# Sharing TensorE clusters from an earlier group on, and placing stores and transposes later in one engine's order

## The chip, the cores and the metric

The kernel runs on one core of a Trainium2 chip. A core has five engines with an instruction stream each: TensorE (PE in the profile; PEld is its weight load), VectorE (DVE), ScalarE (ACT), GpSimd (POOL) and SyncE (SP), which in this kernel issues nearly all transfers. Each engine works through its stream in order. The metric is the time of one execution on the device in microseconds; lower is better. Seven runs of the kernel before have a median of 298.03 us and lie between 296.41 and 298.42.

## What is computed

The program is a retention layer followed by a two-layer network. Inputs q, k, v have 8 batches, 8 heads, 576 positions and a head size of 64; the weights are 512 x 2048 and 2048 x 512. All are float32.

```
scores = (q @ k^T) / sqrt(64)
ret    = (scores * Dmat) @ v          # Dmat[h, i, j] = gamma_h ** (i - j) for i >= j, else 0
x      = ret, heads side by side      # 4608 rows of 512
h      = x @ w_in                     # 4608 x 2048
g      = max(h, 0) ** 2
out    = g @ w_out                    # 4608 x 512
```

## The kernel before

**Units and groups.** The 4608 rows are 36 units of 128 rows: for each pair of batches eight "full" units (four of each batch) and a "tail" unit with the last 64 positions of both. Two units form a group, so there are 18 groups, numbered from 0. Each group goes through retention, then the first product with w_in, then relu and square, then the second product.

**Loads.** Units 0 to 7 (groups 0 to 3) are loaded in pairs and transposed on TensorE. From unit 8 on, `add_load` (line 273) issues k, q and v of each unit on SyncE, with a pool of five buffers of each; `add_unit` (line 347) casts k and q to half precision and multiplies v by decay factors on GpSimd (lines 353 and 365), and a DMA transpose on SyncE (`fx2`, line 376, issued at line 378) makes kqT, which holds k and q with the head size across partitions. Six such buffers exist.

**Retention.** It is done in chunks of 64 positions with a carried state, by small matmuls on 64 x 64 quarters of TensorE (`quad`, line 340). A unit has four parts: scores (k times q, line 561), sums (k times v for the state, line 571), output part 1 (state times q of the first kind, line 607), and output part 2 (masked scores times v and the rest of the state, line 612). VectorE masks the scores (`rT`, line 641), forms the states Rm, stmp and R (lines 660 to 670) and multiplies the output by decay factors into xT (line 702).

TensorE does these parts in clusters, each written as one task of the schedule, between 128-wide matmuls. Line 626 says which form a group has: `return JOIN <= g < last_g`, with `JOIN = 11` at line 228. A group that is not joined has a cluster with its own scores and sums (`fa`, line 727) and a later one with output part 1, a drain and output part 2 (`fb`, line 757). A joined group has a cluster with its output part 1 and the scores of the next group (`f1`, line 739), and one with the sums of the next group and its own output part 2 (`f2`, line 743); there is no drain in it, and the next group has no `fa` of its own. So before the change groups 4 to 10 are not joined, groups 11 to 16 are, and group 17, the last, has its output alone.

**The network.** `add_ff` (line 807) makes 64 matmuls with w_in for a group (line 825, tile ph), relu on ScalarE (line 833, rl), and squares on ScalarE or VectorE (lines 843 and 845, gT). From group 2 on the second product is one level of Strassen's scheme (`add_strassen`, line 878): VectorE forms four sums gS of gT blocks (line 891), TensorE makes seven products of eight matmuls each (line 914, tile po), and ScalarE and VectorE put the results together (lines 927, 937, 988). Each finished unit is stored by SyncE (`store`, line 790; lines 794 and 798), from four o tiles.

**The order.** Every piece of work is added to a `Schedule` (line 16) as a task with an engine, a key, an expected duration, the tasks that it depends on, buffers that it takes (`acq`), and an expected latency to other engines. `emit` (line 42) plays these durations through: an engine that is free takes, of the tasks whose data are expected to be there and whose buffers are free, the one with the lowest key. The order in which tasks are started there is the order in which each engine's instructions are written. On SyncE transposes have key -1, stores -0.5 and loads 0, so a transpose or store that is expected to be ready goes ahead of all loads. On the chip each engine keeps this order and waits for the data themselves.

Of the kernel before, what the change touches and what calls it, by code (L numbers as in the profile page):

```python
# [15 lines left out]
class Schedule:  # L16
# [4 lines left out]
        self.count = dict(count)  # L21
        self.tasks = []

    def add(self, eng, key, dur, fn, deps=(), acq=(), after=None):
        t = dict(eng=eng, key=key, dur=dur, fn=fn, acq=acq, n=len(self.tasks), users=[], free=[],
                 left=len(deps), ready=0.0, lat=self.LAT[eng] if after is None else after)
        for d in deps:
            d["users"].append(t)
        self.tasks.append(t)
        return t  # L30
# [11 lines left out]
    def emit(self):  # L42
        ready = {e: [] for e in self.LAT}
        busy = {e: False for e in self.LAT}
        events = []
        order = []
        seq = 0

        def push(at, what, t):
            nonlocal seq  # L50
            seq += 1
            heapq.heappush(events, (at, seq, what, t))
        for t in self.tasks:
            if t["left"] == 0:
                heapq.heappush(ready[t["eng"]], (t["key"], t["n"], t))
        now = 0.0
        while True:
            for e in ready:
                if busy[e]:
                    continue  # L60
                held = []
                while ready[e]:
                    item = heapq.heappop(ready[e])
                    t = item[2]
                    if all(self.count[r] >= t["acq"].count(r) for r in t["acq"]):
                        for r in t["acq"]:
                            self.count[r] -= 1
                        t["start"] = now
                        order.append(t)
                        busy[e] = True  # L70
                        push(now + t["dur"], "end", t)
                        break
                    held.append(item)
                for item in held:
                    heapq.heappush(ready[e], item)
            if not events:
                break
            now = events[0][0]
            while events and events[0][0] <= now + 1e-9:
                _, _, what, t = heapq.heappop(events)  # L80
                if what == "end":
                    busy[t["eng"]] = False
                    for w in t["users"]:

                        push(now + (0.0 if w["eng"] == t["eng"] else t["lat"]), "dep", w)
                    for g in t["free"]:
                        push(now + t["lat"], "free", g)
                elif what == "dep":
                    t["left"] -= 1
                    if t["left"] == 0:  # L90
                        heapq.heappush(ready[t["eng"]], (t["key"], t["n"], t))
                else:
                    t["left"] -= 1
                    if t["left"] == 0:
                        self.count[t["res"]] += 1
        assert len(order) == len(self.tasks)
        for t in order:
            t["fn"]()
# [3 lines left out]
def kernel(  # L102
# [122 lines left out]
    SQ_ACT = (0, 1, 2, 3, 4, 5, 6)  # L225
    SPREAD = 0.1
    SQ_LATE = (1, 4, 6)
    JOIN = 11
    LAG = {"v2": 1.2, "w1": 1.3, "k4": 0.7, "q4": 0.5}
    PAIRED = 8  # L230
    FIRST = ["k0", "q0", "v0", "k2", "q2", "w0", "v2", "w1", "w2", "w3", "w4", "w5", "w6", "w7", "k4", "q4", "v4", "k6", "q6", "v6"]
    sched = Schedule(dict(ff=4, prS=1, prO=1, g=3, ld=5, wst=4, kq=7, v16=7, rT=4, x=3, rl=3, o=4, p1=2, u2=2, u4=2,
                          R=6, Rm=6, kqT=6))
    add = sched.add
    tile_of = {}
# [99 lines left out]
    T = {}  # L335
# [11 lines left out]
    def add_unit(u, base):  # L347

        kind, b, c = units[u]
        tail = [tail_dec] if kind == "tail" else []  # L350

        def sorted_cast(op, out_, in_):
            op(out=out_.rearrange("p (n b a d) -> p n b a d", n=2, b=2, a=2),  # L353
               in_=in_.rearrange("p (n a b) d -> p n b a d", n=2, a=2))

        def fk():
            t = tile_of["kq", u] = cast.tile([P, 2, H * D], FP16, name="kq16", tag="kq16")
            sorted_cast(nc.gpsimd.tensor_copy, t[:, 0], tile_of["k32", u])

        def fq():  # L360
            sorted_cast(nc.gpsimd.tensor_copy, tile_of["kq", u][:, 1], tile_of["q32", u])

        def fv():
            t = tile_of["v16", u] = cast.tile([P, H, D], FP16, name="v16", tag="v16")
            nc.gpsimd.tensor_tensor(  # L365
                out=t, in0=tile_of["v32", u],
                in1=vdec[kind].rearrange("p (h o) -> p h o", o=1).to_broadcast([P, H, D]), op=ALU.mult)
        ck = add("POOL", base, 0.65, fk, deps=[loaded["k", u]], acq=("kq",))
        cq = add("POOL", base + 1, 0.62, fq, deps=[loaded["q", u], ck])
        cv = add("POOL", base + 2, 1.1, fv, deps=[loaded["v", u]] + tail, acq=("v16",))  # L370
        for what, t in (("k", ck), ("v", cv)):
            for w in gate.get((what, u), []):
                sched.need(w, t)
        T["casts", u] = [ck, cq, cv]
        sched.free("ld", [ck, cq, cv])
        def fx2():
            t = tile_of["kqT", u] = work.tile([P, 2 * NP, P], FP16, name="kqT", tag="kqT", bufs=6)
            nc.sync.dma_start_transpose(out=t, in_=tile_of["kq", u].rearrange("p x n -> p (x n)"))
        T["kqT", u] = [add("SP", -1, 2.7, fx2, deps=[ck, cq], acq=("kqT",), after=3.0)]

    def add_unit_pair(u, base):

# [239 lines left out]
    last_g = len(groups) - 1  # L622
# [167 lines left out]
    def store(u, o, lo=0, hi=DM, eng=nc.sync):  # L790
        kind, b, c = units[u]
        if kind == "full":
            r0 = b * S + c * P
            eng.dma_start(out=out[r0:r0 + P, lo:hi], in_=o[:, lo:hi])
        else:
            for i in range(2):
                r0 = (b + i) * S + 512
                eng.dma_start(out=out[r0:r0 + 64, lo:hi], in_=o[i * 64:(i + 1) * 64, lo:hi])
# [8 lines left out]
    def add_ff(g):  # L807
        us = groups[g]
        n = len(us)
# [8 lines left out]
        for fb in range(NF // nf):  # L818
            for j in range(nf):
                def f(fb=fb, j=j):  # L820
# [3 lines left out]
                    for m in range(NP):  # L824
# [3 lines left out]
                              deps=[T["x", u] for u in us] + wcast_of(nf * fb + j) + f1[-1:],  # L828
                              acq=("ff",) if j == 0 else ()))
# [26 lines left out]
        for s, u in enumerate(us):  # L856
            end = base2 + NF * (s + 1)
            f2 = T["ff2"][-1:] if s == 0 else f2[-1:]
            for fi in range(NF):
                def f(fi=fi, s=s, u=u):  # L860
                    if fi == 0:
                        tile_of["po", u] = ps_ff.tile([P, DM], FP32, name="po", tag="ff")
                    nc.tensor.matmul(tile_of["po", u], lhsT=tile_of["g", g][:, fi, s * P:(s + 1) * P],  # L863
                                     rhs=w_out16[:, fi, :], start=(fi == 0), stop=(fi == NF - 1))
                f2.append(add("PE", base2 + NF * s + fi, 0.216, f, deps=[sq[fi // nf]] + wcast[4 + fi // 4] + f2[-1:],
                              acq=("ff",) if fi == 0 else ()))

            def fo(u=u):
                tile_of["o", u] = o_pool.tile([P, DM], FP32, name="o", tag="o")
                nc.scalar.copy(out=tile_of["o", u], in_=tile_of["po", u])  # L870
            oc = add("ACT", end + 1, 0.59, fo, deps=[f2[-1]], acq=("o",))
            sched.free("ff", [oc])
            st = add("SP", -0.5, 0.7, lambda u=u: store(u, tile_of["o", u]), deps=[oc], after=2.5)
            sched.free("o", [st])
        sched.free("g", [f2[-1]])
        T["ff2"].append(f2[-1])
# [1 line left out]
    def add_strassen(g, us, base, sq):  # L878
# [51 lines left out]
        def o_tile(u):  # L930
            if ("o", u) not in tile_of:
                tile_of["o", u] = o_pool.tile([P, DM], FP32, name="o", tag="o")
            return tile_of["o", u]
# [63 lines left out]
        T["ff2"].append(p4)  # L997
        for u, ds in ((uA, [d11, c12]), (uB, [d22, d21])):
            if g < last_g:
                st = [add("SP", -0.5, 0.7, lambda u=u: store(u, o_tile(u)), deps=ds, after=2.5)]  # L1000
            else:
                st = []
                for d in ds:
                    lo = 0 if d in (d11, d21) else HM
                    eng = ("ACT", base + 25.1, 0.05) if d is d11 or d is d22 else ("SP", -0.5, 0.05)
                    st.append(add(*eng, lambda u=u, lo=lo, eng=eng: store(u, o_tile(u), lo, lo + HM,
                                                                          nc.scalar if eng[0] == "ACT" else nc.sync),
                                  deps=[d], after=2.5))
            sched.free("o", st)
# [44 lines left out]
```

## Time and profile before

| | value |
|---|---|
| median of seven runs | 298.03 us |
| profiled execution | 296.97 us |
| its span | 295.3 us |
| TensorE's granted clock | 0.998 |
| read from memory, written | 36.70 MB, 9.44 MB |
| share of the DMA engines, main queue | 83.1% |

The profile is one execution. The span runs from its first to its last instruction; 1.67 us of the execution lie around it. "Busy" is the time in which an engine has at least one instruction in work, as a share of the span. A row of who waited for whom has the total of the waits, how often, and the longest. In a row of instructions in order of time the first number is the start from the beginning of the span, the second the length of that run, and "x8" the number of instructions in it. The ends of matmuls are modelled, so the price of a group of matmuls is read from start to start.

### The profile page before, as it was taken

To read this page: it belongs to the slowest core of one execution; us is meant where nothing else is said; L and a number is where in the kernel's file an instruction comes from. 1 tells how busy PE (TensorE), PEld (TensorE's weight loads), DVE (VectorE), ACT (ScalarE), POOL (GpSimd) and SP (SyncE) were. 2 spreads that over 40 slices of the span, in tenths; PEclk is the share of its full clock that TensorE was granted. 3 is DMA by queue.
4 is the path that set the end of the run, shared out by engine and by line. 5 is a ranking of instruction groups with operands and counts; after the bars stand their busy time and mean duration, and the time that the engine had idled before them with its cause. 6 is when DMAs were issued, how large, how long until landed. Compare 5 with 4: busy or idle time off the path is not lost.

```text
span 295.3 us, 10076 instructions
## 1 busy us (share of the span) xinstructions
PE 284.3 (96%) x4328; PEld 234.6 (79%) x4328; DVE 200.6 (68%) x433; ACT 183.4 (62%) x347; POOL 95.5 (32%) x129
## 2 busy tenths in 40 slices
PE   7988999999989999999999999999999999999995
PEld 2557666687878888888888888788888888888884
DVE  4777489859494959493949587866668776464732
ACT  6256863485747675767576657657666677657830
POOL 4444374634243405162524232434141520000000
PEclk9999999999999999999999999999999999999999
DMA  7999999899998979899979799999899960201004
GB/s 205 327 372 386 362 259 235 191 224 164 219 172 204 184 161 189 207 195 205 191 174 165 173 173 211 206 169 213 126 230 179 204 163 2 74 2 71 2 0 144
DMA packets 139421, 54.14 MB, mean 183 GB/s; under 512 B 118128, under 2 KB 130928, under 8 KB 139376
## 3 DMA queue, kind: packets, MB, share of 16 engines
q1 hardware_dynamic: 139072, 53.23, 83.1%
q8 instruction: 34, 0.56, 0.9%
q10 hardware_dynamic: 304, 0.26, 0.3%
q14 instruction: 11, 0.09, 0.1%
HBM read 36.70 MB, written 9.44 MB: 156 GB/s over the span
## 4 chain that ended last, share of the span: by engine, by line
PE 79%; DVE 9%; DMA 5%; ACT 4%; issue 1%; POOL 1%; SPq 0%; DVEq 0%
PE ph L825 35%; PE po L914 30%; PE po L863 5%; PE psO L341 4%; DMA wo<-in_moe_w_out_dram 3%; DVE gS L891 3%; ACT gT L843 2%; PE psc L341 2%; DMA pair<-in_q_dram 2%; ACT rl L833 2%; PE psS L341 1%; PE warm L244 1%; PE psT L416 1%; DVE rT L641 1%; DVE R L670 1%
## 5 line engine op out<-in xcount | busy, mean ns | idle before, releaser
L825 PE MATMUL ph<-xT,w_in 128*128 128x256 f16 x1152 | 138.9, 273 | 1.2 <-POOL w_in L320 1.2
L825 PEld LDWEIGHTS <-w_in 128*128 128x128 f16 x1152 | 111.0, 98 | 16.8 <-POOL w_in L320 2.0
L833 ACT ACTIVATE rl<-ph 128x512 f16<-128x512 f32 x144 | 84.2, 588 | 48.3 <-PE ph L825 42.0
L843 ACT ACTIVATE gT<-rl 128x512 f16<-128x512 f16 x104 | 65.6, 631 | 3.1
L914 PEld LDWEIGHTS <-gS 128*128 128x128 f16 x512 | 49.4, 98 | 7.5 <-DVE gS L891 1.7
L914 PE MATMUL po<-wT,gS 128*128 128x256 f16 x384 | 52.1, 273 | 0.9 <-DVE gS L891 0.9
L891 DVE TENSOR_TENSOR gS<-gT 128x512 f16<-128x512 f16 x64 | 35.0, 547 | 20.7 <-ACT gT L843 20.6
L891 DVE TENSOR_TENSOR gS<-gT,gS 128x512 f16<-128x512 f16 x64 | 34.3, 537 | 21.8 <-ACT gT L843 21.1
L365 POOL TENSOR_TENSOR v<-v,vdec_full 128x512 f16<-128x512 f32 x24 | 26.7, 1113 | 62.8 <-DMA v<-in_v_dram 51.2
L914 PEld LDWEIGHTS <-gT 128*128 128x128 f16 x384 | 37.2, 98 | 4.9 <-issue 0.4
L914 PE MATMUL po<-w_out,gT 128*128 128x256 f16 x256 | 34.5, 273 | 0.0
L353 POOL CAST kq<-k 128x512 f16<-128x512 f32 x28 | 19.9, 710 | 28.4 <-DMA k<-in_k_dram 25.0
L845 DVE TENSOR_TENSOR gT<-rl 128x512 f16<-128x512 f16 x40 | 18.9, 475 | 14.8 <-ACT rl L833 14.1
L927 ACT COPY u<-po 128x256 f32<-128x256 f32 x32 | 11.8, 370 | 23.7 <-PE po L914 23.7
L353 POOL CAST kq<-q 128x512 f16<-128x512 f32 x28 | 18.7, 666 | 22.5 <-DMA q<-in_q_dram 22.0
L702 DVE TENSOR_TENSOR xT<-psO,gam_full 128x512 f16<-128x512 f32 x28 | 18.5, 683 | 3.7 <-PE psO L341 3.7
L641 DVE TENSOR_TENSOR rT<-psc,mask 128x512 f16<-128x512 f32 x28 | 18.6, 680 | 1.8 <-PE psc L341 1.8
L937 DVE TENSOR_TENSOR o<-po,u 128x256 f32<-128x256 f32 x31 | 13.0, 418 | 10.0 <-PE po L914 6.2
L914 PE MATMUL po<-wT,gT 128*128 128x256 f16 x128 | 16.6, 273 | 0.4 <-DVE o L937 0.4
L914 PE MATMUL po<-w_out,gS 128*128 128x256 f16 x128 | 16.6, 273 | 0.0
L863 PE MATMUL po<-w_out,gT 128*128 128x512 f16 x64 | 15.6, 379 | 0.2 <-POOL w_out L320 0.2
L937 DVE TENSOR_TENSOR o<-po,p 128x256 f32<-128x256 f32 x17 | 7.1, 419 | 9.3 <-PE po L914 2.9
(79 smaller groups left out, 248.2 us busy)
## 6 DMA issues: line engine op xcount, KB each, us to landing
out_dram<-o SPq DMA_DIRECT2D x31, 256.0 KB, 2.7
k<-in_k_dram SPq DMA_DIRECT2D x24, 256.0 KB, 4.6
q<-in_q_dram SPq DMA_DIRECT2D x24, 256.0 KB, 4.9
v<-in_v_dram SPq DMA_DIRECT2D x24, 256.0 KB, 4.2
wi<-in_moe_w_in_dram SPq DMA_DIRECT2D x4, 1024.0 KB, 9.9
wo<-in_moe_w_out_dram SPq DMA_DIRECT2D x4, 1024.0 KB, 9.4
pair<-in_k_dram SPq DMA_DIRECT2D x4, 512.0 KB, 5.6
pair<-in_q_dram SPq DMA_DIRECT2D x4, 512.0 KB, 6.4
```

Of the source, the lines that this page charges most:

```text
L341: nc.tensor.matmul(out_, lhsT=lhsT, rhs=rhs, start=start, stop=True, skip_group_check=True, tile_position=(64 * row, 64 * col))
L353: op(out=out_.rearrange("p (n b a d) -> p n b a d", n=2, b=2, a=2), in_=in_.rearrange("p (n a b) d -> p n b a d", n=2, a=2))
L365: nc.gpsimd.tensor_tensor(out=t, in0=tile_of["v32", u], in1=vdec[kind].rearrange("p (h o) -> p h o", o=1).to_broadcast([P, H, D]), op=ALU. ...
L641: nc.vector.tensor_tensor(out=r, in0=tile_of["psc", g][:, :, cols(s)].rearrange("p a (n i) -> p a n i", i=64), in1=mask.rearrange("p (o r ...
L825: nc.tensor.matmul(tile_of["ph", g, fb][:, j, :], lhsT=w_in16[:, m, fi * P:(fi + 1) * P], rhs=tile_of["x", g][:, m, :], start=(m == 0), st ...
L833: nc.scalar.activation(out=t, in_=tile_of["ph", g, fb], func=ACTF.Relu)
L843: nc.scalar.activation(out=t, in_=rl, func=ACTF.Square)
L845: nc.vector.tensor_tensor(out=t, in0=rl, in1=rl, op=ALU.mult)
L863: nc.tensor.matmul(tile_of["po", u], lhsT=tile_of["g", g][:, fi, s * P:(s + 1) * P], rhs=w_out16[:, fi, :], start=(fi == 0), stop=(fi == N ...
L891: nc.vector.tensor_tensor(out=Sx(k, h), in0=in0(h), in1=in1(h), op=op)
L914: nc.tensor.matmul(tile_of["pb", g, bank], lhsT=left(i), rhs=right[:, i, :], start=(start and i == 0), stop=(i == HF - 1), skip_group_chec ...
L937: nc.vector.tensor_tensor(out=o_tile(u)[:, half * HM:(half + 1) * HM], in0=bank(x), in1=tile_of[name, g], op=ALU.add)
```

## The change

`Schedule.add` gets a parameter `lag`. A task whose last dependency is expected at some time comes up for selection only `lag` later; nothing is added to the program itself. The DMA transposes of units 8 to 35 get a lag of 1.5, and the stores a lag of 5.0, except those of the last two groups. `JOIN` goes from 11 to 6, so groups 6 to 10 get the joined form too. `JOIN` also sets the keys of the GpSimd casts at line 716, which for groups 7 to 11 fall by L = 32, half the distance of a group's keys to the next.

```diff
-    def add(self, eng, key, dur, fn, deps=(), acq=(), after=None):
-        t = dict(eng=eng, key=key, dur=dur, fn=fn, acq=acq, n=len(self.tasks), users=[], free=[],
+    def add(self, eng, key, dur, fn, deps=(), acq=(), after=None, lag=0.0):
+        t = dict(eng=eng, key=key, dur=dur, fn=fn, acq=acq, n=len(self.tasks), users=[], free=[], lag=lag,
                  left=len(deps), ready=0.0, lat=self.LAT[eng] if after is None else after)
...
                 elif what == "dep":
                     t["left"] -= 1
                     if t["left"] == 0:
-                        heapq.heappush(ready[t["eng"]], (t["key"], t["n"], t))
+                        push(now + t["lag"], "go", t)
+                elif what == "go":
+                    heapq.heappush(ready[t["eng"]], (t["key"], t["n"], t))
...
-    JOIN = 11
+    JOIN = 6
     LAG = {"v2": 1.2, "w1": 1.3, "k4": 0.7, "q4": 0.5}
+    LAG_T, LAG_O = 1.5, 5.0
...
-        T["kqT", u] = [add("SP", -1, 2.7, fx2, deps=[ck, cq], acq=("kqT",), after=3.0)]
+        T["kqT", u] = [add("SP", -1, 2.7, fx2, deps=[ck, cq], acq=("kqT",), after=3.0, lag=LAG_T)]
...
-            st = add("SP", -0.5, 0.7, lambda u=u: store(u, tile_of["o", u]), deps=[oc], after=2.5)
+            st = add("SP", -0.5, 0.7, lambda u=u: store(u, tile_of["o", u]), deps=[oc], after=2.5, lag=LAG_O)
...
-                st = [add("SP", -0.5, 0.7, lambda u=u: store(u, o_tile(u)), deps=ds, after=2.5)]
+                st = [add("SP", -0.5, 0.7, lambda u=u: store(u, o_tile(u)), deps=ds, after=2.5, lag=LAG_O if g < last_g - 1 else 0.0)]
```

## The prediction

> **What bounds the kernel now.** I read the busy shares first, then who TensorE waited for, then busy time by stretches of one group each, and last the order of instructions on TensorE and on SyncE. The busy shares:
>
> ```profile
> PE 284.3 (96%) x4328; PEld 234.6 (79%) x4328; DVE 200.6 (68%) x433; ACT 183.4 (62%) x347; POOL 95.5 (32%) x129
> ```
>
> TensorE is busy nearly always, and the waits of 60 to 196 us add up to little. These are three of them, from the table of who waited for whom:
>
> ```profile
> PE po L914 <- DVE gS L891: 0.9, 2, 0.5
> PE psO L341 <- DVE stmp L666: 0.7, 1, 0.7
> PE po L914 <- DVE o L937: 0.4, 1, 0.4
> ```
>
> No row has TensorE waiting for a load, a store or a transpose in steady state. In the table of busy time by stretches (first the stretch, then its length, then PE's busy time), take four groups with clusters of their own, the group with a stall, and two that share clusters:
>
> ```profile
> 105.30:119.80 14.50, 14.40 (x247) 12.52 (x245) 10.44 (x23) 8.68 (x17) 4.80 (x6) 1.00 0.96 186
> 149.45:165.25 15.80, 15.27 (x255) 13.31 (x253) 11.74 (x23) 11.12 (x21) 4.96 (x6) 1.00 1.00 177
> 210.16:224.50 14.34, 14.33 (x246) 12.31 (x246) 10.78 (x22) 8.78 (x17) 4.61 (x6) 1.00 1.13 196
> ```
>
> The whole length is TensorE's own work at a granted clock of 1.00. A microsecond is won only by taking work off TensorE or by closing one of its few gaps, and lost only by opening a new one.
>
> **The change on TensorE.** Both forms have two clusters of 64-wide matmuls per group. Alone: scores and sums of g (64 quads), later output part 1, a drain, output part 2 (64 quads). Shared: part 1 of g with scores of g+1 (48), later sums of g+1 with part 2 of g (80, no drain). The order of TensorE's instructions shows each one's price; columns are start, length, engine, line, what, count.
>
> ```profile
> 95.56 1.04 PE L914 MATMUL po<-wT,gS 128*128 128x256 f16 x8
> ...
> 97.16 1.05 PE L825 MATMUL ph<-xT,w_in 128*128 128x256 f16 x8
> ...
> 102.85 0.60 PE L825 MATMUL ph<-xT,w_in 128*128 128x256 f16 x4
> ...
> 104.28 1.05 PE L914 MATMUL po<-wT,gT 128*128 128x256 f16 x8
> ```
>
> Back to back, a 256-column matmul takes 0.1093 us (a run of 44 takes 4.80 to 4.81 in the chain). Eight from 95.56 end at 96.43, and wide work resumes at 97.16: the scores cluster costs 0.73. Four from 102.85 end at 103.29, resumption at 104.28: the output cluster costs 0.99. Together 1.72. The shared pair, by the same rows near 205 and 209 us:
>
> ```profile
> 204.26 1.04 PE L914 MATMUL po<-w_out,gT 128*128 128x256 f16 x8
> ...
> 205.72 1.05 PE L914 MATMUL po<-wT,gS 128*128 128x256 f16 x8
> ...
> 208.35 1.04 PE L914 MATMUL po<-wT,gT 128*128 128x256 f16 x8
> ...
> 210.09 3.12 PE L825 MATMUL ph<-xT,w_in 128*128 128x256 f16 x27
> ```
>
> 204.26 + 0.87 = 205.13 to 205.72 is 0.59; 208.35 + 0.87 = 209.22 to 210.09 is 0.87. Together 1.46, so 0.26 less; as the number of quads is the same, this is the drain. The change turns groups 6 to 10 from the first form into the second: 5 x 0.26 = 1.3 us. The period says the same: 90.04 to 149.45 is four groups alone (14.85 each), 195.14 to 253.64 four shared (14.63), 5 x 0.22 = 1.1. I take 1.3, with 1.1 to 1.5 as bounds. The one extra scores cluster at the place where sharing begins exists in both kernels, at group 11 before and at group 6 after.
>
> Here a rule speaks against the change. The Trainium skill, TensorEngine Tiling (Array Packing), section Tiling Modes, says that changing the tiling mode drains TensorE. Counted by it, both forms enter and leave the 64x64 mode twice per group, and nothing would be saved: the sum would be 297.5 (only the gap below). The rows decide, because they contain these switches in both forms and still differ by 0.26.
>
> **The gap at group 10.** In the stretch 149.45 to 165.25 TensorE idles 15.80 - 15.27 = 0.53. The output cluster waits there for VectorE's run of rT, Rm, stmp, R for both units, which begins at 159.03 and ends at 163.8, six microseconds after the scores. A shared output cluster needs only sums finished half a group earlier, and in the shared groups at 195 to 253 us the idle time is 0.0. I count 0.5 gained. The 0.49 at 188.91, where the group that starts sharing loads VectorE with a second set of masks and sums, moves to group 6 at the same price. The gaps of groups 4 and 5 (15.70 - 15.23 = 0.47, 14.80 - 13.98 = 0.82) lie ahead of the change of form; I leave them.
>
> **What sharing asks of the data.** Scores of g+1 now stand in the cluster of g, some 10 us earlier. The trace has room. Group 6's first w_in product starts at 112.09. Ahead of it must come two masks (1.3), the second cluster (0.87), two xT (1.3) and handoffs (about 0.5), plus the first cluster (0.6): it is free as late as 107.5. The transpose of unit 15 is issued at 99.30 and lands 3.9 later (median of the page), at 103.2; with the 1.5 of LAG_T in full, 104.7. Same sum for group 7: product at 126.83, free until 122.3; transpose of unit 17 at 115.16, so 119.1, with lag 120.6. That is the tightest, 1.7 us. Groups 8, 9 and 10 have 2.6, 4.6 and 5.9. So even unimproved loads suffice, and the cost is nothing; beyond these margins each microsecond would be one on TensorE, which has then no other work.
>
> **The change on SyncE's queue.** SyncE issues in order, so whatever waits holds all loads behind it:
>
> ```profile
> 97.19 0.89 SPq L280 DMA_DIRECT2D q<-in_q_dram  x1
> 99.30 1.23 SPq L378 DMA_TRANSPOSE kqT<-kq  x1
> 103.45 1.35 SPq L798 DMA_DIRECT2D out_dram<-o  x2
> 104.90 1.32 SPq L378 DMA_TRANSPOSE kqT<-kq  x1
> 106.32 0.54 SPq L794 DMA_DIRECT2D out_dram<-o  x1
> 106.91 0.42 SPq L280 DMA_DIRECT2D v<-in_v_dram  x1
> ```
>
> From 100.5 to 103.45 it waits for the sums of a store, and the v load is issued only at 106.91. From 45 to 240 us SyncE waits 26.6 us ahead of transposes and 26.7 ahead of stores. LAG_O = 5.0 puts about five microseconds of other issues (loads of 0.4 to 2.0 each) ahead of each store, LAG_T one or two ahead of each transpose. No instruction is added: the same loads, 28 transposes and stores. Loads then leave earlier by roughly the store waits, 2 us a group, if the DMA engines carry it: their busy share is 0.95 to 1.1, with pauses where SyncE waits, so perhaps half. A transpose may go out later by its 1.5 or earlier because its cast is. On TensorE all of it is worth 0, as it waits for none of them; below nothing only past the 1.7 us margin. Stores leave later, but four o tiles are two groups of 14.6 us each, against 5.0 + 2.7 to landing: free. The last two groups' stores have no lag, so the tail from 267 us on is as before.
>
> Casts that come earlier fall on other VectorE work. The Trainium skill, SBUF — State Buffer, section Who interferes with whom, says that a VectorE instruction with two SBUF inputs and a GpSimd one that reads SBUF exclude each other. The trace agrees: a gS takes 0.41 alone and 1.26 at 157.09 beside the v cast of 156.76. Earlier casts only shift such collisions; their number stays. By the rows of shared groups they cost TensorE nothing; by the rule at its worst, in the doubled set of group 6 (two rT of 0.65, two Rm + stmp + R of 1.25, so 3.8 us more VectorE work in an interval of 15 that already has 10 to 11), I bound it at 2 us.
>
> **Sum.** The profiled execution took 296.97, its span 295.3 and 1.67 around it. 296.97 - 1.3 - 0.5 = 295.2. It lies 1.06 below the median of the seven runs, so I forecast 298.03 - 1.8 = **296.2**.
>
> **Rivals.** (a) The forecast, **0.54**, with its own range 295.2 to 297.2 (drain 1.1 to 1.5, gap 0 to 0.8, the new place of the transition costing up to 0.5 more). (b) Earlier data also closes the gaps of groups 4 and 5, another 1.3: 294.9, **0.12**. For it: unit 9's v cast ends at 64.75, just ahead of its use at 65.45. Against: the chain there runs through ScalarE squares and VectorE sums. (c) The gain is eaten at group 6 by VectorE collisions, 2 us: 298.2, **0.16**. Against it: the same transition cost 0.49 before. (d) **Slower, 0.18**: transposes stand behind so many loads that they bind TensorE in groups 6 to 8. It decides once a transpose lands more than 1.7 us later than before plus lag. Three more loads in front at up to 2.0 each make 4 to 6; with TensorE in order the lateness is paid once, about 4 us: 298.0 + 4 - 1.8 = 300.3. For it: margins are smallest where the loads have least lead. Against: SyncE would be freed of up to 26.7 us of waits.
>
> **How the numbers follow.** A measurement of this kernel can tell about 0.5% (1.5 us) from no change, so faster ends at 296.5. Of (a) I put 0.7 below that: 0.38, with (b) 0.50. Same: the rest of (a) and (c), 0.32. Slower: (d), 0.18. The range leaves out (d) alone: 294.6 to 298.8.
>
> **What will show it.** The periods between starts of long w_in runs fall from 14.85 to about 14.6 from group 6 on. SyncE's waits for o fall from 26.7 us to a few. VectorE is nearly full near 100 to 110 us, with about 0.5 of idle TensorE there. Wrong would be: a wait of scores for a transpose or k/q cast between 100 and 140 us; a drain-free cluster that costs more than 0.9; a longer gap for gS at group 6 or 7.

## The result and the profile after

The changed kernel takes 294.93 us (median of 13 runs, 293.88 to 296.23); the kernel before, measured beside it on the same chip, takes 297.28 (median of 34, 296.00 to 298.92). The ratio is 0.9918, with a 95% interval of 0.9901 to 0.9936: about 2.4 us less, where 1.8 were forecast. The profiled execution of the changed kernel took 295.75, which is 0.8 above its own median; its span is 294.0.

The busy shares of the changed kernel:

```profile
PE 283.9 (97%) x4328; PEld 234.9 (80%) x4328; DVE 201.3 (68%) x433; ACT 184.3 (63%) x347; POOL 94.6 (32%) x129
```

TensorE is still what sets the time. Where did the difference arise? Both spans are cut at the start of the same two long runs of matmuls with w_in, that of group 4 and that of group 16. Columns of the table of busy time by stretches: the stretch, its length, then the busy time of PE, PEld, DVE, ACT and POOL, each with its number of instructions, the granted clock, the DMA share, GB/s. Before:

```profile
58.86:90.04 31.18, 29.90 (x475) 25.77 (x475) 23.00 (x43) 19.87 (x39) 11.71 (x14) 1.00 1.00 197
90.04:267.33 177.29, 175.78 (x2887) 152.89 (x2885) 121.86 (x257) 118.32 (x227) 53.16 (x65) 1.00 0.87 165
```

After:

```profile
59.70:89.40 29.70, 29.52 (x474) 25.65 (x475) 20.63 (x43) 19.71 (x38) 11.64 (x16) 1.00 1.09 211
89.40:265.80 176.40, 175.00 (x2886) 152.38 (x2885) 124.10 (x258) 119.31 (x227) 50.49 (x62) 1.00 0.76 160
```

This is not the picture of the forecast. The clusters of groups 6 to 10 lie in the second stretch, and it became only 0.89 us shorter. The first one, where no form of a cluster changed, became 1.48 shorter, 1.10 of it in idle time of TensorE (31.18 - 29.90 = 1.28 before, 0.18 after). Ahead of 59 us the changed kernel is 0.84 later. Two profiles of single executions thus suggest that idle time moved. The experiments had to say which part of the idle time belongs to the change, and which to the execution.

The clusters themselves are as forecast. TensorE of the changed kernel, in order of time:

```profile
102.21 1.47 PE L828 MATMUL ph<-xT,w_in 128*128 128x256 f16 x12
103.77 0.82 PE L917 MATMUL po<-wT,gT 128*128 128x256 f16 x6
...
105.01 0.39 PE L917 MATMUL po<-wT,gT 128*128 128x256 f16 x2
105.24 1.91 PE L828 MATMUL ph<-xT,w_in 128*128 128x256 f16 x16
...
107.85 1.92 PE L828 MATMUL ph<-xT,w_in 128*128 128x256 f16 x16
```

With 0.1093 a matmul, 103.77 + 6 x 0.1093 = 104.43, and wide work resumes at 105.01: 0.58 for the first shared cluster. 105.24 + 1.75 = 106.99 to 107.85: 0.86 for the second. Together 1.44, against 1.46 in the forecast. Also, a gap of 0.25 stands ahead of 103.77.

A larger gap follows some six microseconds later, at 113.97 (113.10 + 0.87), where the next matmuls start at 115.05:

```profile
113.10 1.04 PE L828 MATMUL ph<-xT,w_in 128*128 128x256 f16 x8
115.05 0.61 PE L917 MATMUL po<-wT,gS 128*128 128x256 f16 x4 [0.91 <-DVE gS L894]
```

What was VectorE doing, on which TensorE waits there? VectorE first, then GpSimd, of the same execution:

```profile
112.83 0.82 DVE L848 TENSOR_TENSOR gT<-rl 128x512 f16<-128x512 f16 x1
113.69 1.31 DVE L894 TENSOR_TENSOR gS<-gT,gS 128x512 f16<-128x512 f16 x1
...
116.75 0.41 DVE L894 TENSOR_TENSOR gS<-gT 128x512 f16<-128x512 f16 x1
```

```profile
112.76 0.62 POOL L356 CAST kq<-q 128x512 f16<-128x512 f32 x1
113.67 1.04 POOL L368 TENSOR_TENSOR v<-v,vdec_full 128x512 f16<-128x512 f32 x1 [0.29 <-DMA v<-in_v_dram]
```

A gS that takes 0.41 alone takes 1.31 beside a v multiplication of 1.04. The forecast had seen such a pair and given it no price in its sum.

SyncE, finally, does not wait less. Its waits from 45 to 240 us in the changed kernel (total, times, longest):

```profile
SPq L797 <- ACT o L991: 21.2, 10, 3.2
SPq L381 <- POOL kq L356: 17.6, 10, 3.6
SPq L381 <- POOL v L368: 16.3, 12, 2.3
SPq L797 <- DVE o L940: 14.8, 8, 10.4
```

With the small rows, stores wait 41.2 us (26.7 before) and transposes 33.9 (26.6 before). The loads did go out earlier, and so did the transposes: those of units 15, 17, 19, 21 and 23 are issued at 90.5, 104.1, 120.8, 133.6 and 148.2, and before at 99.3, 115.2, 129.2, 142.1 and 156.1. That is 8 to 11 us of lead, and it seems that SyncE waits more because it is ahead.

### The profile page after: what moved, and what is told of

The parts are those of the page before. It is cut to its first block, busy times and chain, and to the rows that moved or that the text cites. A ratio compares the mean times of both kernels' runs of the same rounds, so it can differ in the third digit from the quotient of the medians.

```text
span 294.0 us, 10070 instructions
## 1 busy us (share of the span) xinstructions
PE 283.9 (97%) x4328; PEld 234.9 (80%) x4328; DVE 201.3 (68%) x433; ACT 184.3 (63%) x347; POOL 94.6 (32%) x129
## 4 chain that ended last, share of the span: by engine, by line
PE 78%; DVE 8%; DMA 6%; SPq 2%; ACT 2%; issue 2%; POOL 1%; DVEq 0%; POOLq 0%
PE ph L828 36%; PE po L917 31%; PE psO L344 4%; DMA pair<-in_v_dram 3%; DMA wo<-in_moe_w_out_dram 3%; PE po L866 3%; SPq L298 2%; PE psc L344 2%; PE psS L344 2%; DVE wT L779 1%; ACT rl L836 1%; DVE gS L894 1%; ACT gT L846 1%; DVE R L673 1%; DVE gT L848 1%
## 5 line engine op out<-in xcount | busy, mean ns | idle before, releaser
L894 DVE TENSOR_TENSOR gS<-gT,gS 128x512 f16<-128x512 f16 x64 | 36.6, 575 | 13.3 <-ACT gT L846 12.7
L356 POOL CAST kq<-k 128x512 f16<-128x512 f32 x28 | 19.3, 688 | 65.5 <-DMA k<-in_k_dram 58.7
L894 DVE TENSOR_TENSOR gS<-gT 128x512 f16<-128x512 f16 x64 | 31.0, 484 | 13.0 <-ACT gT L846 12.8
L368 POOL TENSOR_TENSOR v<-v,vdec_full 128x512 f16<-128x512 f32 x24 | 25.8, 1076 | 18.9 <-DMA v<-in_v_dram 15.6
L848 DVE TENSOR_TENSOR gT<-rl 128x512 f16<-128x512 f16 x40 | 20.8, 523 | 14.5 <-ACT rl L836 14.1
```

The source lines that it names most:

```text
L368: nc.gpsimd.tensor_tensor(out=t, in0=tile_of["v32", u], in1=vdec[kind].rearrange("p (h o) -> p h o", o=1).to_broadcast([P, H, D]), op=ALU. ...
L848: nc.vector.tensor_tensor(out=t, in0=rl, in1=rl, op=ALU.mult)
L894: nc.vector.tensor_tensor(out=Sx(k, h), in0=in0(h), in1=in1(h), op=op)
```

## The experiments

My theory at this point: the drains give 1.3 us, and the lags move only transfers that TensorE never waits for. Rivals: the lags carry the gain and sharing none; or sharing needs the lead that the lags give to the loads. After the first four runs a third question came up: are the gaps that come and go collisions of VectorE with GpSimd (both at work at once, and one stretched by the other), or do they follow from the order of the instructions, as the forecast said of group 10? All diffs are against the changed kernel unless they say otherwise.

### Sharing without the lags

```diff
-    LAG_T, LAG_O = 1.5, 5.0
+    LAG_T, LAG_O = 0.0, 0.0
```

> JOIN = 6 with both lags at 0. Theory A (the gain is TensorE's: five drains less and a looser VectorE chain, while loads, stores and transposes are hidden): about the same gain as the whole change, 2.4 us, so 294.5 to 295.5 against a kernel before of 297.3. Theory B (sharing from group 6 needs the lead that the lags give to the loads): TensorE waits for a transpose or a cast between 100 and 140 us, half of the gain or more is gone, 296.5 or slower.

Measured: 297.59 beside 297.40 for the kernel before; ratio 1.0008 (0.9980 to 1.0036). Sharing alone gains nothing. (`JOIN` moves the keys of the casts as well; no run separates the two.) The five drains are gone, but TensorE has new gaps at the place where sharing starts:

```profile
104.04 3.22 PE L828 MATMUL ph<-xT,w_in 128*128 128x256 f16 x28
...
112.61 1.04 PE L917 MATMUL po<-wT,gS 128*128 128x256 f16 x8
114.40 1.05 PE L828 MATMUL ph<-xT,w_in 128*128 128x256 f16 x8 [0.76 <-DVE xT L705]
116.88 0.61 PE L917 MATMUL po<-w_out,gS 128*128 128x256 f16 x4 [1.43 <-DVE gS L894]
```

The first shared cluster begins at 104.04 + 28 x 0.1093 = 107.10, against 104.43 in the changed kernel. Then TensorE idles from 113.48 to 114.40 (0.92, for xT) and from 115.27 to 116.88 (1.61, for gS). So the cluster comes too late for what hangs on it, although its data are there: the transpose of unit 15 was issued at 98.70, and landings in this trace take at most 5.1 us.

### The lags without sharing

```diff
-    JOIN = 6
+    JOIN = 11
```

> The lags as in the change, JOIN left at 11. Theory A: TensorE waits for no transfer, so only the places of its gaps shift: 296.8 to 297.8, no change that can be told from none. Theory B: a part of the gain shows here, through the gaps of groups 4 and 5 (1.3 us): 295.5 to 296.3.

Measured: 296.02 beside 297.40; ratio 0.9947 (0.9930 to 0.9964). The lags alone gain 1.6 us by the ratio (1.4 by the medians), in a kernel where no matmul between 45 and 240 us waits for a load or a store. This was not foreseen: all steps of the forecast had put the lags at zero.

### Sharing with one lag of the two

The stores' lag alone:

```diff
-    LAG_T, LAG_O = 1.5, 5.0
+    LAG_T, LAG_O = 0.0, 5.0
```

> JOIN = 6 and the lag of the stores, none for the transposes. Theory A: as the whole change, 294.5 to 295.5. Theory B: the stores are what held the loads back, so this too is near the whole change, and the kernel with the transposes' lag alone is not.

The transposes' lag alone:

```diff
-    LAG_T, LAG_O = 1.5, 5.0
+    LAG_T, LAG_O = 1.5, 0.0
```

> JOIN = 6 and the lag of the transposes, none for the stores. Theory A: as the whole change, 294.5 to 295.5. Theory B: loads still stand behind waiting stores, so 296.5 or slower.

Measured beside 297.40: 295.59, ratio 0.9933 (0.9911 to 0.9955), and 295.40, ratio 0.9939 (0.9916 to 0.9962). Each lag by itself brings most of the gain, and their intervals can't be told apart. With the stores' lag alone the first shared cluster stays at 107.30, as late as without lags, and with the transposes' lag alone it moves to 105.64. So there are two ways of gaining here, and an earlier cluster is only one of them. The two lags differ early on: the long w_in run near 59 us starts at 59.3 to 59.6 in all seven profiles with LAG_O and at 58.8 to 59.1 in all seven without it, those of the later experiments included. The stores' lag costs about 0.5 us there, by a way that stays open.

### The kernel before, profiled again

No edit, one more execution of the kernel before.

> The kernel before, unchanged, for a second profile. If the gaps of groups 4, 5 and 10 belong to its order, they are there again with 0.5, 0.8 and 0.5; if they come and go with the times at which loads land, they differ by half or more.

It took 296.71, span 295.0. The gaps of the first profile at groups 4, 5 and 10 are not there. In the first profile the last R of group 10 had been stretched, beside a v multiplication:

```profile
162.67 1.15 DVE L670 TENSOR_TENSOR R<-stmp,dec 128x256 f16<-128x256 f32 x1
162.50 1.04 POOL L365 TENSOR_TENSOR v<-v,vdec_full 128x512 f16<-128x512 f32 x1 [1.52 <-PE po L914]
```

The second execution has another gap, at 116.49 (115.62 + 0.87). TensorE, VectorE and GpSimd of it:

```profile
115.62 1.04 PE L914 MATMUL po<-w_out,gS 128*128 128x256 f16 x8
...
118.67 1.03 PE L914 MATMUL po<-wT,gT 128*128 128x256 f16 x8 [0.26 <-DVE o L937]
```

```profile
114.71 1.26 DVE L670 TENSOR_TENSOR R<-stmp,dec 128x256 f16<-128x256 f32 x1
...
117.40 0.88 DVE L670 TENSOR_TENSOR R<-stmp,dec 128x256 f16<-128x256 f32 x1
```

```profile
114.65 1.04 POOL L365 TENSOR_TENSOR v<-v,vdec_tail 128x512 f16<-128x512 f32 x1 [0.88 <-DMA v<-in_v_dram]
...
117.39 0.62 POOL L353 CAST kq<-q 128x512 f16<-128x512 f32 x1 [0.91 <-DMA q<-in_q_dram]
```

From 116.49 to 118.67 are 2.18 us for an output cluster that costs 0.99 to 1.02 where nothing is stretched: 1.2 us of idle TensorE, at a place where the first profile had none. R, which takes 0.42 alone, is stretched twice. The instructions and their order are the same in both executions; what differs is where GpSimd's work, which starts when a load lands, meets VectorE's. So those gaps are a property of an execution and not of the order alone. A gap that stays can be a collision too: at group 11, where sharing starts in the kernel before, TensorE stands still for 0.65 in the first execution (from 188.26) and for 0.47 and 0.22 in the second (from 186.67 and 188.46), with stretched VectorE work just ahead of it both times.

### GpSimd work that hardly reads

To take the collisions away without touching any order, GpSimd's three instructions per unit from unit 8 on convert 8 columns only and fill the other 504 of each row with a constant; the conversion of the rest and the decay factors of v are left out. One such pair takes 0.24 + 0.52 = 0.76 us, where a cast of k took 0.71, so the data come at about the same time: the transpose of unit 15 leaves at 98.27, before at 99.30. First in the order of the kernel before:

```diff
-    JOIN = 6
+    JOIN = 11
-    LAG_T, LAG_O = 1.5, 5.0
+    LAG_T, LAG_O = 0.0, 0.0
...
+        def fill_only(out_, in_):
+            nc.gpsimd.tensor_copy(out=out_[:, 0:8], in_=in_[:, 0, 0:8])
+            nc.gpsimd.memset(out_[:, 8:], 0.01)
...
-            sorted_cast(nc.gpsimd.tensor_copy, t[:, 0], tile_of["k32", u])
+            fill_only(t[:, 0], tile_of["k32", u])
-            sorted_cast(nc.gpsimd.tensor_copy, tile_of["kq", u][:, 1], tile_of["q32", u])
+            fill_only(tile_of["kq", u][:, 1], tile_of["q32", u])
-            nc.gpsimd.tensor_tensor(
-                out=t, in0=tile_of["v32", u],
-                in1=vdec[kind].rearrange("p (h o) -> p h o", o=1).to_broadcast([P, H, D]), op=ALU.mult)
+            fill_only(t.rearrange("p h d -> p (h d)"), tile_of["v32", u])
```

> JOIN = 11 and no lags, as the kernel before, but the GpSimd casts of k, q and v of units 8 to 35 read only 8 columns of the load and fill the rest with a constant: the conversion of k, q, v and the decay factors of v are left out. Theory C (the gaps of groups 4, 5 and 10 are VectorE work stretched by GpSimd instructions that read SBUF at the same time): gS and R go back to 0.41 each everywhere, these gaps close, and the time falls by 1.5 to 2.5 us to 295 to 296. Theory D (the gaps come from the order of VectorE's work or from late data): nothing to 0.7 us.

Measured: 294.48 beside 297.53; ratio 0.9895 (0.9867 to 0.9922). Its five runs lie between 294.40 and 294.76. The costliest groups of VectorE, of this kernel and then of the kernel before (busy in us, mean in ns, then the idle time before):

```profile
L896 DVE TENSOR_TENSOR gS<-gT 128x512 f16<-128x512 f16 x64 | 27.0, 421 | 20.9 <-ACT gT L848 20.6
L896 DVE TENSOR_TENSOR gS<-gT,gS 128x512 f16<-128x512 f16 x64 | 26.9, 422 | 21.9 <-ACT gT L848 21.3
```

```profile
L891 DVE TENSOR_TENSOR gS<-gT 128x512 f16<-128x512 f16 x64 | 35.0, 547 | 20.7 <-ACT gT L843 20.6
L891 DVE TENSOR_TENSOR gS<-gT,gS 128x512 f16<-128x512 f16 x64 | 34.3, 537 | 21.8 <-ACT gT L843 21.1
```

The gS are back at 0.42 us, and between 45 and 240 us no matmul has a wait in the table of waits, neither at group 10 nor at group 11 nor anywhere else. GpSimd is still busy for 84.5 us (95.5 before), so what went is mostly its reading and not its work. Collisions cost the kernel before about 3 us of its 297, in amounts that differ from run to run.

The same GpSimd work with sharing, without lags (the second `LAG_T, LAG_O` line and `fill_only` as above, `JOIN = 6`):

```diff
-    LAG_T, LAG_O = 1.5, 5.0
+    LAG_T, LAG_O = 0.0, 0.0
```

> The same casts without reading, with JOIN = 6 and no lags. Theory C: the 2.5 us of gaps between 109 and 117 us that ate the gain of sharing come from stretched gS and R, so this kernel is faster than the one with JOIN = 11 by the drains, 1.3, and stands near 294. Theory D: the clusters of group 6 stand too late in TensorE's order, so that xT and the sums of group 7 come while TensorE has nothing else; the gap stays near 2 us, and the kernel is not faster than the one with JOIN = 11.

Measured: 294.48 beside 297.53; ratio 0.9894 (0.9867 to 0.9922). Equal to the one without sharing. Summing the price of every cluster from 48 to 270 us in both traces gives 25.5 us apart and 24.1 shared, so the drains are worth 1.4. What takes their place? TensorE and VectorE of this kernel:

```profile
108.55 1.04 PE L919 MATMUL po<-wT,gS 128*128 128x256 f16 x8
...
112.05 1.04 PE L919 MATMUL po<-wT,gS 128*128 128x256 f16 x8
113.17 1.05 PE L830 MATMUL ph<-xT,w_in 128*128 128x256 f16 x8
114.75 0.61 PE L919 MATMUL po<-w_out,gS 128*128 128x256 f16 x4 [0.54 <-DVE gS L896]
```

```profile
107.44 1.28 DVE L646 TENSOR_TENSOR rT<-psc,mask 128x512 f16<-128x512 f32 x2
...
110.57 0.69 DVE L707 TENSOR_TENSOR xT<-psO,gam_full 128x512 f16<-128x512 f32 x1 [0.39 <-PE psO L344]
111.18 0.41 DVE L667 TENSOR_TENSOR Rm<-psS,R 128x256 f16<-128x256 f32 x1
111.63 0.43 DVE L671 TENSOR_TENSOR stmp<-psS,Rm 128x256 f32<-128x256 f32 x1
112.09 0.42 DVE L675 TENSOR_TENSOR R<-stmp,dec 128x256 f16<-128x256 f32 x1
112.43 0.68 DVE L707 TENSOR_TENSOR xT<-psO,gam_full 128x512 f16<-128x512 f32 x1
```

Gaps of 0.25 (ahead of 113.17) and 0.71 (ahead of 114.75) remain without any collision, and one of 0.62 elsewhere: 1.58, which eats the 1.4. The cluster begins at 106.64, the second xT ends at 113.11 and the first product that needs it starts at 113.17. That is a chain of 6.5 us. Between the two xT stands the first unit's Rm, stmp and R (1.25). Ahead of them the second cluster begins at 109.42 (108.55 + 0.87), 0.7 after the masks are done (107.44 + 1.28 = 108.72), because wide matmuls stand before it in TensorE's order. gS comes behind the second unit's Rm, stmp and R.

With everything, the same GpSimd work with sharing and both lags (`fill_only` as above, no other edit):

```diff
-            sorted_cast(nc.gpsimd.tensor_copy, t[:, 0], tile_of["k32", u])
+            fill_only(t[:, 0], tile_of["k32", u])
```

> The casts that fill with a constant and hardly read (conversion of k, q, v and the decay factors of v left out), now with JOIN = 6 and both lags. Theory E (without lags the shared clusters of group 6 stand about 3 us too late in TensorE's order, and the 1.6 us of gaps at 113, 114 and 126 us that remain without collisions come from that; the lags bring the loads forward and with them the clusters): these gaps are gone, and the time is 1.3 to 1.6 us below the 294.48 of the two kernels without lags, 292.9 to 293.2. If the lags act only through collisions, the time stays at 294.5.

Measured: 293.51 (five runs, 293.48 to 293.79) beside 297.22; ratio 0.9874 (0.9850 to 0.9898). The first shared cluster begins at 104.11, and the gaps of both earlier kernels, 0.91 for gS in the changed kernel among them, are gone. So without collisions sharing plus lags gains 294.48 - 293.51 = 0.97, less than expected by about the early 0.5 of the stores' lag, and the changed kernel loses 294.93 - 293.51 = 1.4 to collisions, where the kernel before loses about 3. The 0.97 rests on five runs each, beside different runs of the kernel before, and the intervals of the two ratios overlap; but the traces give the same. TensorE's stops between wide matmuls (clusters, and gaps over 0.1) from 48 to 270 us add up to 25.5 without sharing and without lags, and to 24.0 here: 1.5, less the 0.5. The same sum is 28.3 and 27.7 in the two profiles of the kernel before and 26.3 in the changed kernel's. What is left of the span is 267.0 to 267.4 in all seven profiles without the stores' lag and 267.6 to 267.8 in all seven with it, so these stops and that early cost make up the whole difference to within 0.4 us.

### A drain put back

```diff
             def f2():
                 emit_sums(g + 1, "prS")
+                nc.tensor.drain()
                 emit_out2(g)
```

> The changed kernel with a drain put between the sums of the next group and output part 2, in all eleven shared clusters. If the drain is what sharing saves, each second cluster goes from 0.87 to about 1.13 and the time rises by 11 x 0.26 = 2.9 us over the changed kernel, to 297.5 to 298. If the count of changes between 128-wide and 64-wide work is the price, nothing changes: 295.

Measured: 298.88 beside 297.53; ratio 1.0048 (1.0031 to 1.0066). TensorE:

```profile
104.95 1.91 PE L829 MATMUL ph<-xT,w_in 128*128 128x256 f16 x16
...
107.85 1.92 PE L829 MATMUL ph<-xT,w_in 128*128 128x256 f16 x16
```

104.95 + 1.75 = 106.70, to 107.85 are 1.15 where the cluster without a drain took 0.86 to 0.87: 0.28 for one drain, in each of eleven groups, 3.1 us. By the two ratios (1.0048 and 0.9918) the kernel is 1.3% or 3.9 us slower than the changed one. Between the two profiled executions it is 298.74 - 295.75 = 3.0; both have other gaps of the kind that differs between runs, 2.1 us here (0.84 at 142.7, 0.41 and 0.83) and 1.8 there. The 0.8 us beyond the drains is not explained.

### The cluster moved earlier by other means

The planner takes a transpose to last 2.7 on SyncE and to be usable 3.0 later. The traces show 1.23 for the issue and 3.9 to the landing. Here only these two planning numbers are shortened and the lags are zero:

```diff
-    LAG_T, LAG_O = 1.5, 5.0
+    LAG_T, LAG_O = 0.0, 0.0
...
-        T["kqT", u] = [add("SP", -1, 2.7, fx2, deps=[ck, cq], acq=("kqT",), after=3.0, lag=LAG_T)]
+        T["kqT", u] = [add("SP", -1, 1.3, fx2, deps=[ck, cq], acq=("kqT",), after=2.6, lag=LAG_T)]
```

> JOIN = 6, no lags, real casts; only the planner's numbers for a transpose are shortened from 2.7 + 3.0 to 1.3 + 2.6, about what the trace shows. Theory E says that the place of the cluster follows from when the planner expects the data. Half of the lateness of 3 us is the planner's own: the first shared cluster stands at about 105.5 instead of 107.1, and the time is about 1 us below sharing without lags, 296 to 297. If the place follows from the loads alone, it stays at 107 and the time at 297.5.

Measured: 294.68 (five runs, 294.24 to 294.98) beside 297.22; ratio 0.9910 (0.9881 to 0.9938). TensorE:

```profile
101.62 0.60 PE L828 MATMUL ph<-xT,w_in 128*128 128x256 f16 x4
...
102.66 0.61 PE L828 MATMUL ph<-xT,w_in 128*128 128x256 f16 x4
```

The first shared cluster now begins at 101.62 + 0.44 = 102.06, earlier than expected, and this kernel has the whole gain without a lag. What the planner expects of the transpose decides where TensorE's cluster is written. The lags move it too, it seems by bringing loads, and with them the expected transposes, forward; no run shows the planner's own times. The 2.9 us gained on sharing without lags (297.59) are more than the 1.58 of gaps that the late cluster cost without collisions, so a part seems to be collisions that fell otherwise. No run separates it. In time this kernel can't be told from the changed one (their ratio intervals overlap).

### Sharing from one and from two groups earlier

```diff
-    JOIN = 6
+    JOIN = 5
```

> The changed kernel with JOIN = 5. One drain less is 0.26; against it, the loads of groups 5 and 6 have less lead, so the place of the first shared cluster may cost up to 1 us. 294.5 to 296.

```diff
-    JOIN = 6
+    JOIN = 4
```

> The changed kernel with JOIN = 4, two drains less, 0.5. Unit 9's data are ready only just ahead of their use, and the scores of units 10 and 11 are now asked for 10 us earlier: the first shared cluster comes late and gaps of 1 to 3 us follow. 295 to 297.5.

Measured beside 297.22: 295.41, ratio 0.9933 (0.9908 to 0.9958), and 296.24, ratio 0.9970 (0.9946 to 0.9994). Another saved drain each should have given 0.26 and 0.52. Instead gaps return at the first shared cluster: 0.53 at 96.45 with 5, and 0.58 at 83.5 and 0.71 at 84.95 with 4. With 5 the kernel is within noise of the changed one, with 4 it is worse. I read this as a price of the transition where its transposes have little lead, but it is one profile each.

## Why the forecast came out as it did

**The drain: right.** 0.26 a group was read from two pairs of clusters; 1.4 for five groups was measured by the sums, and 0.28 by putting one back. The rule that changing the tiling mode drains TensorE (the Trainium skill, TensorEngine Tiling (Array Packing), section Tiling Modes) gave 0 for this step; an explicit drain costs 0.28 beside whatever the switches cost.

**The gap of group 10: wrong.** The 0.53 was put down to an order in which the output cluster waits for rT, Rm, stmp and R. A second execution with the same order has no such gap, and the kernel without collisions has it neither. The chain exists, but it fits unless GpSimd stretches it, as it stretched the last R (1.15 for 0.42).

**The transition at the same price: wrong.** Forecast 0.5, from a gap at group 11 that is itself a collision: without reads it is gone, in the same order. In the profile of the changed kernel the gap is 1.08 and is a collision: it is gone in the kernel with all lags and no reads. Without lags it is 0.25 + 0.71 + 0.62 even with no collision, and without lags and with collisions 0.92 + 1.61 and more. The price depends on where the cluster stands.

**"Even unimproved loads suffice": wrong,** and twice. First, I compared landing times on the chip with the time of need, and they do hold; but the place of the cluster in TensorE's order comes from the planner's expected times, and by these, without lags, it stands at 107.10 instead of 104.43. Second, I held the cluster free until 107.5 on a chain of 4.6 us. It measures 6.5 without collisions: the first unit's Rm, stmp and R (1.25) between the two xT were left out, and so were the 0.7 for which the second cluster stands behind wide matmuls. The lags are no decoration of sharing; with the planner's numbers as they are, it is worth nothing without them (1.0008).

**SyncE's waits: wrong in sign,** right in consequence. The waits for stores rose from 26.7 to 41.2 us. That loads leave earlier is right, with 8 to 11 us at the transposes where I had counted one to two a group: a lead won early seems to add up from group to group.

**"Earlier casts only shift collisions; their number stays": right on VectorE, wrong in the price.** The Trainium skill, SBUF — State Buffer, section Who interferes with whom, was cited for the exclusion and the trace agreed. VectorE's busy time, which every stretched instruction lengthens, is 200.6 and 205.7 us in the two profiles of the kernel before, 200.8 with the lags alone, 201.3 in the changed kernel, and 182.5 to 183.9 without reads. So about as much is stretched as before. What I had set at nothing in the sum is its cost to TensorE: about 3 us before and 1.4 after, so 1.5 of the 2.4 us gained come from here. A stretched gS or R costs only where a product is due that needs it, and with the lags the stretches must fall at better places. Why they do stays open. In the first five microseconds after each long w_in run has begun, when VectorE has little work of two inputs, GpSimd's work does grow (from 6.1 and 6.8 us in the two profiles before to 11.0 with the lags alone, 13 runs each), but the stretch of gS, gT and R in the six that follow doesn't fall (15.0 and 19.7 before, 14.9 with the lags).

**The sum.** In medians: kernel before 297.3 = 294.5 without collisions + about 3; changed kernel 294.93 = 293.51 + 1.4. Some 1.0 us come from the order (1.4 of drains less an early cost of the stores' lag of about 0.5) and 1.5 from collisions. The forecast's 1.8 was 1.3 + 0.5; the second term was a misread gap, and a larger one that was set at zero took its place. That the sum came close to 2.4 is therefore in good part luck. So is the match of rival (b), 294.9: the gaps of groups 4 and 5 that it closes are gone from the changed kernel's profile, but also from the second profile of the kernel before. A gain eaten by VectorE at group 6 is what happens without lags, in part by collisions and in part by the late cluster. The slower rival, transposes behind loads, did not occur: with lags they leave earlier. (Its sum, 298.0 + 4 - 1.8, is 300.2 and not 300.3.)

## What to carry to other kernels

Before a gap in one profile is charged to the order of instructions, profile a second execution of the same kernel: a gap that moves does not come from the order alone, and its price is an average over runs. A gap that stays proves nothing yet; here only GpSimd work without reads told the one at group 11 from an order. Where a planner writes the order, ask what it expects and not only what the chip does; a piece that is ready in the trace can still stand late, since nothing on the chip moves it forward. Give a change that brings work closer together (here a shared cluster) its lead in the same step, and sum the chain behind it with every instruction that its engine has in between.

## What was not expected of the hardware

The scatter of this kernel's times seems to be mostly that of its collisions between GpSimd and VectorE. With GpSimd instructions that hardly read, the five runs of each of three kernels lie within 0.3 to 0.4 us (294.40 to 294.76, 294.29 to 294.70, 293.48 to 293.79); the 15 runs of the kernel before that stood beside the last of them lie between 296.21 and 298.29, the 13 of the changed one within 2.4 us. Five runs with all reads lie within 0.7 us (the shortened transpose) and 0.9 (sharing from group 5), so a part of the difference is the number of runs. A 0.42 us gS beside a 1.04 us v multiplication ends 1.31 after its start: it stands still for nearly the whole of the other's time.
